# Moving the third group's logs forward and interleaving the first group's second layer in a gated-attention and feed-forward kernel

## Chip, cores and metric

One Trainium2 chip, one core. The metric is the device time of one execution in microseconds (us). The kernel before was run three times without a profile; one more execution was profiled, and all lines of the trace come from that one. Engines: PE (TensorE, matmul; PEld is its weight load), ACT (ScalarE), DVE (VectorE), POOL (GpSimd), SP (SyncE, which issues most DMAs).

## The reference

Two blocks. The first is a recurrence over 768 time steps for 4 batches and 8 heads of dimension 48, with a complex decay per step and channel; the second takes the first's output as 3072 rows of 384 and runs a two-layer network with the activation h cos(h).

```python
mag = np.sqrt(a_re * a_re + a_im * a_im)
scale = np.minimum(mag, 0.999) / (mag + 1e-06)
a_re_n, a_im_n = (a_re * scale, a_im * scale)
for t in range(S):
    new_re = ar * S_re - ai * S_im
    new_im = ar * S_im + ai * S_re
    kv = np.einsum('bhd,bhe->bhde', k[:, :, t], v[:, :, t])
    S_re, S_im = (new_re + kv, new_im)
    y[:, :, t] = np.einsum('bhd,bhde->bhe', q[:, :, t], S_re)
...
h = x @ w_in          # 384 -> 2048
g = h * np.cos(h)
return (g @ w_out)    # 2048 -> 384
```

The inputs q, k, v, a_re, a_im are float32; the two weight matrices arrive as 64-bit floats.

## The kernel before

**Tiling.** The time axis is cut into chunks of 128 steps: 6 per batch, 24 in all (n = 0 to 23). Two chunks make a group (g = 0 to 11). Everything of a group is worked on together: its tiles are 128 steps by 768 values. Within a chunk the recurrence is replaced by attention: with P the running product of the decay's magnitudes and its phase the running sum of its angles, the keys are divided and the queries multiplied by P times cosine and sine, and scores under a causal mask do the rest; a state of 96 x 48 per head passes from chunk to chunk.

**The steps of a group**, by their names in the code:

- `log_steps` (called by `logs`): squares of a_re and a_im on ACT, their sum on DVE, then logarithms and exponentials on ACT with DVE steps between: eight DVE steps in all for groups from 2 on. They end with the tile `tan` (tangent of the half angle) and with the log of the magnitude, which groups from 2 on split into an upper and a lower part (`hi`, `lo`). The last reader of a_re is a check on ACT; after it the a_re and a_im loads of the group after may land, as there is one buffer for each. `logs` yields the logs and then these loads.
- `p_powers`: a running sum over the 128 steps by a matmul with a triangle of ones (PE, `lgs`), one per chunk, then Exp on ACT to P and 1/P (`Q`). In groups from 2 on it takes two records of PE per chunk, for `hi` and `lo`.
- `g_angle`: arctan on ACT, which needs another table of ACT than Ln and Exp.
- `prods`: `g_carry` (adds the last phase of the group before, and splits the angle into `hi` and `lo`), then `p_even` and `p_apply` (DVE: five products; SP: the row DMA of P's last step, and two loads of it).
- `g_phase`: the running sum of angles (PE, `phs`), one per chunk. In groups 0 and 1 the second matmul of a chunk takes the finished phase of the chunk before. ACT casts the sum to a whole number of turns, and DVE subtracts it.
- `keys`: `g_trig` (sine and cosine on ACT; the sine goes where P was, so it waits for the row DMA), `g_stack` (four DVE products to `ks` and `qs`), and then, from group 2 on, `f_transpose` for kT and qT: a DVE transpose of 32 x 32 blocks, then DMAs through DRAM. In group 1 `turned` does it with PE.
- `chunks`: per chunk the scores (`f_scores`, two halves with a DVE mask behind each), the state (`f_state`) and the outputs (`f_out`); at the end `f_xt`, DMAs that bring the group's result into the shape of the network's input `xT`, and the loads of k, q and v for the group after the next.
- `first`: the first layer, `mm1` for jp = 0 to 7. Each unit is six matmuls of 128 x 256 (12 records of PE) into one of three PSUM buffers, then `mm1_gate`: sine and square on ACT, product on DVE. The buffer comes free with the product.
- `second`: the second layer of groups 0 and 1, `mm2(g, i, j0, 4)`: four quarters for each of the two chunks, each quarter four of the 16 blocks of w_out (8 records of PE). Groups from 2 on use another form, with seven products instead (`products`).

**Weights.** w_in and w_out are each fetched in eight raw pieces by POOL's queue into four buffers and converted by `as_floats`: three DVE steps and one of ACT per piece. `convert` makes the steps of this; a piece of w_out (`back`) holds two of the 16 blocks, so a quarter needs two pieces. The raw buffer of a piece comes free when the piece four before it is converted.

**What sets the order.** `weave` takes lists of steps, each with a stretch lo to hi; step i of m gets the place lo + (hi - lo)(i + 0.5)/m, and the steps are emitted in order of place. PE's instructions are chained in the order in which they are emitted (`matmul` and `chain`), and so are ACT's special functions, table loads and squares. The other instructions of ACT and DVE, and the DMAs, are put in order by the scheduler, which works from the order of emission and from when it expects their inputs. On the chip each queue then runs in its compiled order. The change is in the lines from 1284 to 1303, in the function `fast_path`.

Of the kernel before, what the change touches and what calls it, by code (L numbers as in the profile page):

```python
# [487 lines left out]
def fast_path(ctx, tc, q, k, v, a_re, a_im, moe_w_in, moe_w_out, out, least, odd, wide):  # L488
# [11 lines left out]
    G = 2  # L500
# [217 lines left out]
    def cut(t, i, n):  # L718
        return (flat(t) if len(t.shape) == 4 else t)[:, ds(i * DM, n * DM)]
# [116 lines left out]
    def g_angle(g, i, n):  # L836

        at = cut(X[g]["tan"], i, n)
        special(out=at, in_=at, func=AF.Arctan)
# [303 lines left out]
    def products(g, lo, hi):  # L1143
        if g < PLAIN:
            return []
        return [lambda p=p, part=part: seventh(g, p, part)
                for p in range(lo, hi) for part in range(2)]
# [4 lines left out]
    def weave(*parts):  # L1152

        items = []
        for p, (part, lo, hi) in enumerate(parts):
            part = list(part)
            items += [(lo + (hi - lo) * (i + 0.5) / len(part), p, t)
                      for i, t in enumerate(part)]
        for _, _, t in sorted(items, key=lambda x: x[:2]):
            t()  # L1160
# [4 lines left out]
    def keys(g):  # L1165

        if not 0 <= g < NG:
            return
        for i, n in spans(g):
            yield lambda i=i, n=n: g_trig(g, i, n)  # L1170
            yield lambda i=i, n=n: (g_stack(g, i, n), p_end(g, i, n))
            for name in "kT", "qT":
                if g >= PEG:
                    yield lambda i=i, n=n, name=name: f_transpose(g, i, n, name)
# [4 lines left out]
    def powers(g):  # L1179
        return [lambda i=i: p_powers(g, i) for i in range(G)]  # L1180

    def prods(g):
        if not 0 <= g < NG:
            return
        if g not in (1, 2):
            yield from powers(g)
            yield lambda: g_angle(g, 0, G)
        yield lambda: g_carry(g)
        yield lambda: (p_even(g, 0, G), p_apply(g, 0, G))

    def logs(g):
        yield from each(g_log, g)
        if 0 <= g and g + 1 < NG:
            yield lambda: load(g + 1, ("re", "im"))

    def phases(g):
        return [lambda i=i: g_phase(g, i) for i in range(G)] if 0 <= g < NG else []

    def chunks(g):
        for n in range(g * G, g * G + G):  # L1200
            for hh in range(2):
                yield lambda n=n, hh=hh: f_scores(n, hh)
            yield lambda n=n: f_state(n)
            yield lambda n=n: f_out(n)
        yield lambda: f_xt(g)
        if g + 2 < NG:
            yield lambda: load(g + 2, ("k", "q", "v"))

    def first(g):
        order = range(NJ // 2) if g < PLAIN else (0, 4, 1, 5, 2, 6, 3, 7)  # L1210
        return [lambda jp=jp: mm1(g, jp) for jp in order]

    def second(g, i):
        return [lambda j0=j0: mm2(g, i, j0, 4) for j0 in range(0, NJ, 4)] if g < PLAIN else []

    def convert(parts):
        return [lambda dst=dst, src=src: weight(dst, src)() for dst, src in parts]
# [12 lines left out]
    into, back = weight_parts()  # L1230
# [47 lines left out]
    def sums(g, lo, hi):  # L1278
        return [lambda jp=jp: mm1_sums(g, jp) for jp in range(lo, hi)]

    def gates(g, lo, hi):
        return [lambda jp=jp: mm1_gate(g, jp) for jp in range(lo, hi)]

    later = convert(into[RAW:])
    for t in (sums(0, 0, 2) + [lambda: g_angle(1, 0, G)] + later[:1] + gates(0, 0, 1)
              + sums(0, 2, 3) + gates(0, 1, 2) + phases(1) + later[1:2] + gates(0, 2, 3)):
        t()
    weave((first(0)[3:], 0.0, 1.0), (later[2:], 0.0, 0.5), (prods(1), 0.1, 0.12),
          ([lambda: load(2, ("k", "q"))], 0.13, 0.14),
          (keys(1), 0.3, 0.8), (convert(back[:1]), 0.9, 1.0))  # L1290
    over = [t for i in range(G) for name in ("kT", "qT") for t in turned(1, i, name)]
    weave((over, 0.0, 0.2), (chunks(1), 0.2, 1.0), (convert(back[1:4]), 0.1, 1.0))
    weave((second(0, 0), 0.0, 0.25), (convert(back[4:]), 0.0, 0.2), (logs(2), 0.2, 0.21),
          (second(0, 1), 0.25, 0.5), (powers(2), 0.33, 0.36),
          ([lambda: g_angle(2, 0, G)], 0.37, 0.38), (prods(2), 0.38, 0.4),
          (phases(2), 0.44, 0.5), (keys(2), 0.5, 0.65), (first(1), 0.5, 1.0))
    room.close()
    stage.update(pool=ctx.enter_context(tc.tile_pool(name="late", bufs=1)), bufs=1)
    for n in range(2, NG):
        weave((mixes(n - 1, 2, 4), 0.0, 0.12), (logs(n + 1), 0.0, 0.02), (chunks(n), 0.0, 0.36),  # L1300
              (second(n - 1, 0), 0.0, 0.38), (products(n - 1, 0, 3), 0.0, 0.36),
              (prods(n + 1), 0.25, 0.27), (second(n - 1, 1), 0.4, 0.56),
              (products(n - 1, 3, 7), 0.4, 0.56), (phases(n + 1), 0.44, 0.54),
              (keys(n + 1), 0.53, 0.66), (quarters() if n == PLAIN else [], 0.4, 0.9),
              (last_quarter() if n == PLAIN else [], 0.9, 1.0), (first(n), 0.56, 1.0),
              (mixes(n, 0, 2), 0.9, 1.0), (guarded(n - 1, per) if n > 3 else [], 0.1, 0.9))
# [77 lines left out]
```

## Time and profile before

| | us |
|---|---|
| median of 3 runs | 688.53 |
| lowest and highest | 687.56, 688.77 |
| the profiled execution | 685.76 |
| span of its instructions | 684.0 |
| PE busy | 652.7 (95% of the span) |
| DVE busy | 491.0 (72%) |
| ACT busy | 394.0 (58%) |
| POOL busy | 28.9 (4%) |

The granted clock of PE over the whole span is 0.986 of full speed. In a line of a timeline the columns are the start in us from the first instruction, the length in us, the engine, the line of the code (often that of a helper, as L686 for every matmul), the operation, the tile written, the tiles read, their shape and the count of instructions put together; in brackets is how long the engine was idle ahead of it, and what ended that. SPq means SP's own queue of DMA issues. A float32 matmul shows as two records of PE.

The places of the work in the trace: the first layer of group 0 runs from 45 to 72 us, chunks 2 and 3 (group 1) from 72 to 86, the second layer of group 0 with the logs, powers and phases of group 2 from 86 to 122, the first layer of group 1 from 122 to 144, and from there the loop over groups 2 to 11 begins, some 54 us for each.

### The profile page before, as it was taken

The page shows a single profiled execution, that of the slowest core. Times are in us where ns is not written, and L with a number is a line of the kernel's source. Part 1 is how long each engine was busy: PE and PEld are TensorE (multiplying, and loading weights), DVE is VectorE, ACT ScalarE, POOL GpSimd, SP SyncE. Part 2 cuts the span into 40 slices and gives each one's busy share as a digit, 9 for nine tenths or more (in the row PEclk, how much of TensorE's full clock was granted, in tenths as well). Part 3 has the DMA queues.
Part 4 walks back from the last instruction along what each step waited for, and adds up shares of the span by engine and source line. Part 5 has one row for each costly group of instructions (what it writes and reads, how often), then busy time and mean ns, then how long its engine had stood idle before and what let it go on. Part 6 is the DMA issues. An engine that isn't in the chain of part 4 may idle for free.

```text
span 684.0 us, 10721 instructions
## 1 busy us (share of the span) xinstructions
PE 652.7 (95%) x4053; PEld 577.9 (84%) x4053; DVE 491.0 (72%) x793; ACT 394.0 (58%) x728; POOL 28.9 (4%) x47
## 2 busy tenths in 40 slices
PE   7898987979999999999999999999999999999996
PEld 5686944757789989989889989999999999999896
DVE  4999975738768768878768868868768868762241
ACT  6885935474359358459359359359369368342230
POOL 2011100000000001001001000000000000000000
PEclk9999988999999999999999999999999999999999
DMA  9978552453572765675675765665765763363100
GB/s 246 198 195 197 183 161 58 117 126 69 117 184 48 155 170 138 141 185 138 151 174 140 157 168 139 158 168 139 184 140 141 185 149 106 94 145 117 40 6 24
DMA packets 232810, 94.90 MB, mean 139 GB/s; under 512 B 208798, under 2 KB 221217, under 8 KB 232748
## 3 DMA queue, kind: packets, MB, share of 16 engines
q1 hardware_dynamic: 226252, 68.62, 44.5%
q0 software_dynamic: 5632, 25.17, 11.2%
q8 instruction: 34, 0.56, 0.3%
q10 hardware_dynamic: 864, 0.33, 0.2%
q14 instruction: 28, 0.23, 0.1%
HBM read 69.28 MB, written 24.81 MB: 138 GB/s over the span
## 4 chain that ended last, share of the span: by engine, by line
PE 80%; DMA 6%; ACT 6%; DVE 6%; issue 2%; SPq 0%; ACTq 0%; DVEq 0%
PE hp L686 31%; PE op L686 16%; PE sum L686 14%; PE sc L686 6%; PE yp L686 5%; PE sp L686 4%; DMA raw<-in_moe_w_out_dram 3%; PE phs L686 2%; PE lgs L686 1%; DVE mag L675 1%; ACT tan L706 1%; DMA qT<-moved 1%; PE yr L686 1%; DVE w_out L675 1%; ACT rs L706 1%
## 5 line engine op out<-in xcount | busy, mean ns | idle before, releaser
L686 PE MATMUL hp<-xT,w_in 128*128 128x256 f32 x1152 | 251.5, 379 | 1.2 <-DVE gate L675 0.7
L686 PEld LDWEIGHTS hp<-xT,w_in 128*128 128x128 f32 x1152 | 218.3, 190 | 32.2 <-DVE gate L675 1.3
L706 ACT ACTIVATE gate<-hp,half_pi_b 128x512 f32<-128x512 f32 x96 | 65.9, 686 | 125.2 <-PE hp L686 125.2
L686 PE MATMUL op<-w_out,gate 128*128 128x192 f32 (+1 forms) x448 | 109.0, 391 | 3.3 <-DVE w_out L675 3.3
L675 DVE TENSOR_TENSOR gate<-hp,gate 128x512 f32<-128x512 f32 x96 | 65.5, 683 | 55.0 <-ACT junk L675 55.0
L686 PEld LDWEIGHTS op<-w_out,gate 128*128 128x128 f32 x448 | 78.4, 196 | 23.8 <-issue 7.0
L675 ACT ACTIVATE junk<-hp 128x512 bf16<-128x512 f32 x96 | 56.6, 590 | 0.0
L686 PE MATMUL sum<-t_s,s 128*128 128x192 f32 x320 | 55.4, 326 | 0.0
L686 PE MATMUL sc<-qT,kT 96*128 96x128 f32 x384 | 49.4, 276 | 5.5 <-issue 3.9
L686 PEld LDWEIGHTS sc<-qT,kT 96*128 96x128 f32 x384 | 47.5, 192 | 7.8 <-issue 4.5
L686 PEld LDWEIGHTS sum<-t_s,s 128*128 128x128 f32 x320 | 52.5, 190 | 0.3 <-DVE ot L675 0.3
L675 DVE TENSOR_TENSOR atm<-sc,causal 128x512 f32<-128x512 f32 x48 | 33.0, 687 | 23.0 <-PE sc L686 22.9
L675 ACT ACTIVATE ot<-sum 128x192 f32<-128x192 f32 x30 | 9.5, 320 | 49.6 <-PE sum L686 49.6
L686 PE MATMUL yp<-atm,v 128*48 128x128 f32 x352 | 33.6, 277 | 0.7 <-DVE atm L675 0.7
L675 DVE SCALAR_TENSOR_TENSOR ot<-op,ot 128x192 f32<-128x192 f32 x31 | 10.9, 353 | 32.3 <-ACT ot L675 23.7
L702 ACT ACT_TABLE_LOAD x24 | 30.8, 1283 | 4.0 <-DMA ident<-ident_const 3.6
L675 ACT CAST tan<-phs 128x384 int32<-128x384 f32 x24 | 11.5, 478 | 32.1 <-PE phs L686 32.1
L686 PEld LDWEIGHTS sp<-v,ks 128*96 128x96 f32 x320 | 29.7, 165 | 0.0
L686 PE MATMUL sp<-v,ks 128*96 128x48 f32 x320 | 29.6, 245 | 0.0
L686 PE MATMUL yp<-qT,state 96*48 96x128 f32 x304 | 29.6, 272 | 0.0
L686 PE MATMUL sum<-w_out,gate 128*128 128x192 f32 x160 | 29.6, 329 | 0.0
L686 PE MATMUL op<-t_a,gate 128*128 128x192 f32 x160 | 29.0, 332 | 0.0
(138 smaller groups left out, 992.2 us busy)
## 6 DMA issues: line engine op xcount, KB each, us to landing
moved<-tr SPq DMA_DIRECT2D x20, 768.0 KB
raw<-in_moe_w_in_dram POOLq DMA_DIRECT2D x16, 768.0 KB, 5.4
raw<-in_moe_w_out_dram POOLq DMA_DIRECT2D x16, 768.0 KB, 4.9
kT<-moved SPq DMA_DIRECT2D x40, 192.0 KB
qT<-moved SPq DMA_DIRECT2D x10, 768.0 KB
k<-in_k_dram SPq DMA_DIRECT2D x24, 192.0 KB
q<-in_q_dram SPq DMA_DIRECT2D x24, 192.0 KB
v<-in_v_dram SPq DMA_DIRECT2D x24, 192.0 KB
```

Source lines behind the costliest of these rows:

```text
L675: ins = getattr(self.engine, op)(**kw)
L686: chain(nc.tensor.matmul(out, **kw), "tensor")
L702: chain(nc.scalar.preload_act_table_set(table))
L706: chain(nc.scalar.activation(func=func, **kw))
```

## The change

Four things, all in the order of emission; no instruction is added or left out.

1. Opening: the phase sum of group 1's first chunk (`phases(1)[:1]`) is emitted ahead of the first gate and of the third unit's sums, instead of behind the second gate; that of the second chunk stays behind the second gate.
2. `logs(2)` (with the loads of group 3's a_re and a_im behind it) goes from the second layer of group 0, at 0.2, into the weave of group 1's chunks, at 0.7: behind the scores of chunk 3 and ahead of its state.
3. The two chunks of group 0's second layer are interleaved in quarters (`both`): first quarter of chunk 0, first quarter of chunk 1, second quarter of chunk 0, and so on. The last four conversions of w_out, group 2's powers, arctan, products, phases and keys get new places. On PE the order becomes: five quarters, power sums, three quarters, phase sums, first unit of group 1's first layer. Before it was: five quarters (four of chunk 0, one of chunk 1), a power sum, a quarter, a power sum, a quarter, a phase sum, a quarter, a phase sum. Both transposes of `keys(2)` are now emitted ahead of the second unit of the first layer; before, the second transpose came behind it, and the sine and cosine came ahead of the first unit's gate.
4. In the loop the second layer of a group's first chunk goes from 0 to 0.38 to -0.08 to 0.28. This concerns group 1 alone, as later groups have no such steps: its first quarter now comes ahead of group 2's first scores, and the others come earlier as well.

```diff
-    for t in (sums(0, 0, 2) + [lambda: g_angle(1, 0, G)] + later[:1] + gates(0, 0, 1)
-              + sums(0, 2, 3) + gates(0, 1, 2) + phases(1) + later[1:2] + gates(0, 2, 3)):
+    for t in (sums(0, 0, 2) + [lambda: g_angle(1, 0, G)] + later[:1] + phases(1)[:1]
+              + gates(0, 0, 1) + sums(0, 2, 3) + gates(0, 1, 2) + phases(1)[1:] + later[1:2]
+              + gates(0, 2, 3)):
         t()
...
-    weave((over, 0.0, 0.2), (chunks(1), 0.2, 1.0), (convert(back[1:4]), 0.1, 1.0))
-    weave((second(0, 0), 0.0, 0.25), (convert(back[4:]), 0.0, 0.2), (logs(2), 0.2, 0.21),
-          (second(0, 1), 0.25, 0.5), (powers(2), 0.33, 0.36),
-          ([lambda: g_angle(2, 0, G)], 0.37, 0.38), (prods(2), 0.38, 0.4),
-          (phases(2), 0.44, 0.5), (keys(2), 0.5, 0.65), (first(1), 0.5, 1.0))
+    weave((over, 0.0, 0.2), (chunks(1), 0.2, 1.0), (convert(back[1:4]), 0.1, 1.0),
+          (logs(2), 0.7, 0.71))
+    both = [t for pair in zip(second(0, 0), second(0, 1)) for t in pair]
+    weave((both, 0.0, 0.5), (convert(back[4:]), 0.0, 0.3), (powers(2), 0.3, 0.34),
+          ([lambda: g_angle(2, 0, G)], 0.35, 0.36), (prods(2), 0.36, 0.4),
+          (phases(2), 0.47, 0.53), (keys(2), 0.53, 0.6), (first(1), 0.5, 1.0))
...
-              (second(n - 1, 0), 0.0, 0.38), (products(n - 1, 0, 3), 0.0, 0.36),
+              (second(n - 1, 0), -0.08, 0.28), (products(n - 1, 0, 3), 0.0, 0.36),
```

## The prediction

> **What bounds the kernel now.** I count groups and chunks from zero: the second group is group 1, and it has chunks 2 and 3. The profiled execution took 685.76 us: a span of 684.0 and 1.76 around it. It lies 2.77 below the median of the runs, 688.53, so I make the sum against 685.76 and add 2.77 at the end. I read the busy time by stretch first.
>
> ```profile
> 86.00:122.20 36.20, 28.89 (x78) 15.68 (x75) 23.81 (x30) 15.73 (x23) 1.19 (x1) 0.86 0.39 107
> 122.20:148.00 25.80, 21.32 (x98) 17.91 (x96) 15.23 (x19) 14.56 (x30) 0.00 (x0) 1.00 0.66 154
> ...
> 182.20:236.00 53.80, 53.80 (x347) 49.98 (x346) 42.27 (x65) 31.11 (x59) 0.00 (x0) 1.00 0.51 117
> ...
> 100.00:105.00 5.00, 5.00 (x9) 2.55 (x8) 2.39 (x3) 3.69 (x6) 0.00 (x0) 0.54 0.11 39
> ```
>
> The columns are the stretch, its length, each engine's busy time, then the granted TensorE clock. From 182.2 on PE is busy all of the 53.80 us of a group, so that part is bound by PE and whatever is won earlier reaches the end. The stretch from 86.0 to 122.2 (the second layer of group 0) holds 28.89 us of PE work in 36.20 us, part of that at a clock of 0.54; from 122.2 to 148.0, 21.32 us in 25.80. The time that can be had lies here. The order of PE's work over time says where:
>
> ```profile
> 57.80 0.91 PE L686 MATMUL phs<-tan,last 128*128 128x384 f32 x2 [2.88 <-DVE tan L675]
> 58.55 13.28 PE L686 MATMUL hp<-xT,w_in 128*128 128x256 f32 x60
> ...
> 86.12 8.01 PE L686 MATMUL op<-w_out,gate 128*128 128x384 f32 x24
> 96.88 2.07 PE L686 MATMUL op<-w_out,gate 128*128 128x384 f32 x4 [2.75 <-DVE w_out L675]
> 99.48 6.67 PE L686 MATMUL op<-w_out,gate 128*128 128x384 f32 x12 [0.53 <-DVE w_out L675]
> ...
> 115.98 0.44 PE L686 MATMUL phs<-hi,exact 128*128 128x384 f32 x1 [2.06 <-ACT hi L675]
> ...
> 117.27 4.33 PE L686 MATMUL op<-w_out,gate 128*128 128x384 f32 x8
> ...
> 122.22 10.52 PE L686 MATMUL hp<-xT,w_in 128*128 128x256 f32 x48
> 133.40 10.78 PE L686 MATMUL hp<-xT,w_in 128*128 128x256 f32 x48 [0.65 <-DVE gate L675]
> 148.07 1.21 PE L686 MATMUL sc<-qT,kT 96*128 96x128 f32 x8 [3.90 <-issue]
> 149.08 4.40 PE L686 MATMUL op<-w_out,gate 128*128 128x384 f32 x8
> 153.31 1.06 PE L686 MATMUL sc<-qT,kT 96*128 96x128 f32 x8
> ...
> 157.44 0.43 PE L686 MATMUL yp<-atm,v 128*48 128x128 f32 x4 [0.74 <-DVE atm L675]
> ```
>
> The columns are start, time to the end of the piece, instruction and count; in brackets the idle time ahead. PE waits 2.88 us for a phase at 57.80, 2.75 for converted w_out at 96.88, 2.06 for the upper half of group 2's angle at 115.98, and 3.90 at 148.07 (the profile names no releaser; the scores read keys and queries that come by DMA). The clock adds to that: 24 records of a quarter type take 8.01 us at 86.12, 0.334 each, but 12 take 6.67 at 99.48, 0.556 each. A quarter (four of the sixteen blocks of a chunk) is 8 records, 2.67 us.
>
> Then VectorE, ScalarE and the queues of SyncE and GpSimd, which have to feed these places:
>
> ```profile
> 32.52 0.94 DVE L675 TENSOR_TENSOR lg<-lg,tan 128x768 f32<-128x768 f32 x1
> ...
> 48.29 0.95 DVE L675 SCALAR_TENSOR_TENSOR tan<-tan,im 128x768 f32<-128x768 f32 x1
> ...
> 56.59 0.69 DVE L675 TENSOR_TENSOR gate<-hp,gate 128x512 f32<-128x512 f32 x1 [0.92 <-ACT junk L675]
> 57.20 0.55 DVE L675 TENSOR_TENSOR tan<-phs,tan 128x384 f32<-128x384 f32 x1
> ...
> 65.32 0.95 DVE L675 CUSTOM_DVE_ANT_0 w_in<-raw,w_in 128x1536 uint16<-128x1536 uint16 x1
> ...
> 95.40 0.56 DVE L675 TENSOR_SCALAR w_out<-raw 128x768 uint32<-128x768 uint32 x1 [2.05 <-DMA raw<-in_moe_w_out_dram]
> ...
> 97.61 0.95 DVE L675 TENSOR_TENSOR lg<-lg,tan 128x768 f32<-128x768 f32 x1
> 98.48 0.95 DVE L675 CUSTOM_DVE_ANT_0 w_out<-raw,w_out 128x1536 uint16<-128x1536 uint16 x1
> ...
> 106.96 0.95 DVE L675 SCALAR_TENSOR_TENSOR lo<-lg,hi 128x768 fp32r<-128x768 f32 x1
> ...
> 108.81 0.96 DVE L675 SCALAR_TENSOR_TENSOR tan<-tan,im 128x768 f32<-128x768 f32 x1
> ...
> 126.29 0.96 DVE L675 TENSOR_TENSOR ks<-Q,lg 128x768 f32<-128x768 f32 x1 [2.13 <-ACT lg L706]
> ...
> 130.45 2.24 DVE L675 STREAM_TRANSPOSE tr<-ks 128x1536 f32<-128x1536 f32 x1
> ...
> 133.27 2.24 DVE L675 STREAM_TRANSPOSE tr<-qs 128x1536 f32<-128x1536 f32 x1
> ```
>
> ```profile
> 79.09 0.89 ACT L743 ACTIVATE tan<-im 128x768 f32<-128x768 f32 x1
> ...
> 111.38 0.49 ACT L706 ACTIVATE lg<-lgs 128x384 f32<-128x384 f32 x1 [2.06 <-PE lgs L686]
> ...
> 125.41 0.84 ACT L706 ACTIVATE lg<-tan 128x768 f32<-128x768 f32 x1 [2.51 <-DMA row<-lg]
> ```
>
> ```profile
> 86.84 1.19 SPq L1007 DMA_DIRECT2D x<-yT  x2
> ...
> 91.06 0.38 SPq L1011 DMA_DIRECT2D xT<-x  x1
> ...
> 106.05 2.04 SPq L567 DMA_DIRECT2D re<-in_a_re_dram  x4
> ...
> 122.80 0.55 SPq L818 DMA_DIRECT2D row<-lg  x1
> ...
> 140.76 1.30 SPq L911 DMA_DIRECT2D qT<-moved  x1
> ```
>
> ```profile
> 88.37 1.19 POOL L616 DMA_DIRECT2D raw<-in_moe_w_out_dram  x1 [3.33 <-DVE w_out L675]
> ```
>
> Group 2's squares are done on ScalarE at 79.98, but VectorE adds them only at 97.61, after nearly all of the weight conversion: 17.6 us in which the logs could have run. Their eight VectorE steps then last until 109.77, and powers, arctan, phases and first layer all stand behind that. The last raw piece of w_out is asked for at 88.37, lands at 95.40, and is converted at 99.43.
>
> **The change, part by part.**
>
> *Opening.* The first chunk's phase sum goes ahead of the third unit of the first layer (a unit is 12 records, 10.52 / 4 = 2.63 us). While PE does that unit, ScalarE's cast and VectorE's subtraction are made, so the wait of 2.88 at 57.80 goes. What is late next is VectorE: the 60 records from 58.55 are five units, the fourth of which starts at 58.55 + 3 x 2.63 = 66.4, and the conversion of its weights ends at 66.27. That unit had 0.1 us to spare, so PE cannot move up by 2.9 unless VectorE does. VectorE gets back its idle 0.92 at 56.59 (the gate there stands behind less), and the 0.55 of the subtraction at 57.20 moves to an earlier place: I take 1.5, between 0 (the idle time only moves) and 2.9. Everything to 86.12 comes 1.5 earlier: the second layer starts at 84.6.
>
> *Logs.* Nothing is added; eight VectorE steps (seven of 0.95, one of 0.55, 7.2 us by duration, about 0.08 less each back to back) and ScalarE's special functions move from 97.6 onwards to 78.5 onwards, among the masks and conversions. The nearest row for a log stage beside conversions is group 1's own: first addition at 32.52, last step ending at 49.24, 16.7 us. By that group 2's logs end at 78.5 + 16.7 = 95.2; by group 2's own 12.2 us (97.61 to 109.77) at 90.7. They are not wanted before the power sums, at 99.0 by the next part, so both ends cost nothing directly. What they cost is VectorE time: conversions behind them come up to 6.6 us later, less the wait of 2.05 ahead of 95.40, which they fill: 99.43 - 1.5 + 6.6 - 0.9 (the addition stood ahead already) - 2.05 = 101.6 for the last piece.
>
> The loads of the next group's a_re and a_im are moved with the logs. They wait on SyncE's in-order queue for the last reader of a_re. Behind that queue stand the two writes of x and the read of xT (91.06). If the ten issues (about 0.5 each, by the four at 106.05) got ahead of x, x would leave near 100 and xT, 4.2 behind it (86.84, 91.06), near 104; the first layer wants it at 110.3, and the nearest transfer bound, queries asked for at 140.76 and used at 148.07, is 7.3 us. That could cost 1; I expect x to be placed first, because its data are ready when the chunk ends, at about 85, ten us ahead of the logs' end, and cost it at nothing.
>
> *Second layer interleaved.* Same 64 records; 10 records of power and phase sums stand among them, of the same 128x384 shape. At 0.334 that is 24.7 us instead of the 36.10 from 86.12 to 122.22. A quarter of w_out is now used twice before the next is needed, so the needs are spread: order of PE is five quarters, power sums, three quarters, phase sums. Start 84.6; five quarters, 98.0; I add 1.0 of waits for a conversion (0 to 5), 99.0; power sums 1.3, 100.3; the seventh quarter needs the seventh piece at 103.0 and the last piece at 104.3, against 101.6 above: 2.7 to spare where PE waited 2.75 before. Three quarters end at 108.3. The powers' Exp began at 111.38 and the angle's sum at 115.98: 4.6. So its operand is there at 104.9, under cover of those quarters by 3.4, and the wait of 2.06 goes. Phase sums 2.0: the first layer of group 1 starts at 110.3 instead of 122.22. Of these 11.9 us, 10.4 are this part's.
>
> *Keys of group 2 and first layer of group 1.* Sin ran at 125.41, 9.4 us after the angle's operand; it waits for the row DMA that stands at 122.80 behind the moved k and q loads on SyncE. That chain is kept: 104.9 + 9.4 = 114.3. Key products 0.9 later, 115.2 (126.29 against 125.41); four products of 0.95, 3.5 us back to back, and then, as the change puts both transposes ahead of the second unit's gate, 2 x 2.2 us (130.45, 133.27): 123.1. The second gate follows, done at 123.8. The fifth unit needs its buffer and would start at 110.3 + 4 x 2.63 = 120.8: a new wait of 3.0, where 133.40 shows 0.65 now. The eight units end at 123.8 + 10.5 = 134.3. A quarter of group 1's second layer now fills the place where PE waited 3.90: 137.0. From the end of the queries' transpose (135.51) to the scores (148.07) it is 12.6 us: 123.1 + 12.6 = 135.7, so the scores no longer wait. They take 1.0: 138.0. Before, scores and that quarter were both done at 153.31. Gain so far 15.3, of which 3.4 are this part's. What the clock does at the new wait is open. After the wait of 2.88 the 60 records ran in 13.28, 0.221 each, full speed; after 2.75 and 0.53 close together, 12 records lost 12 x 0.222 = 2.7. I take 0.5, nearer the single wait.
>
> The Trainium skill, "TensorE: Matmul & The Clock Gate", section "Why this matters for your kernels", says to leave no gap above some 3 us between matmul bursts, since an idle window halves the clock; it speaks against the new wait. The trace agrees in kind: 0.54 behind the waits of 2.75 and 0.53. An estimate from that page's window of 3.4 us, run at half rate, is a price of 1.7; the forecast would then be 1.2 higher.
>
> *Group 1's second layer.* Three quarters come earlier among the scores. The wait of 0.74 for a mask at 157.44 is covered by a quarter that now stands between scores and outputs: 0.6.
>
> Sum: 1.5 + 10.4 + 3.4 - 0.5 + 0.6 = 15.4; 685.76 - 15.4 = 670.4, and with 2.77, **673.1**.
>
> **The rivals.**
>
> *VectorE becomes the bound (0.20).* Its queue is in order: if its log steps stand there waiting for ScalarE, conversions move by the log stage's 12.2, not by 6.6: the last piece at 107.2 where 104.3 is wanted, a wait of 2.9, with 2.7 for the clock. For it: at 95.40 the conversion of one piece waited for the DMA of the next. Against: conversions that are ready can be queued in the gaps. Gain 9.8: 678.7.
>
> *The change does not do what it says (0.08).* The steps were emitted early enough on ScalarE before, and VectorE still took the addition at 97.61. If the compiled order leaves them there, the power sums wait in PE's order for the lower half, ready at 107.91 - 1.5 = 106.4 instead of 99.0: 7.4 and 2.7 of clock. Gain 5.3: 683.2. Against: the logs are now emitted ahead of the last five conversions.
>
> *More than that (0.11).* The opening gives all 2.9, no conversion waits and the second gate gets ahead of a transpose: 15.4 + 1.4 + 1.0 + 1.5 = 19.3: 669.2.
>
> *The clock stays down: slower (0.05).* Place: the interleaved quarters. If short waits for conversions recur, one per quarter, all 74 records run at 0.556 (+16.4) and the first four units at the same ratio (+7.0): 8.0 slower than before, 696.5. It decides from 69 slow records on, which cancel the 15.4. For it: 99.48, 117.27 (8 in 4.33) and 149.08 (8 in 4.40) all ran slow after waits. Against: each lasted 7 us at most.
>
> Other mishaps that cancel the gain within 0.2% (some 1.4 us, about what a measurement of this kernel can tell from no change): 0.03. The forecast keeps 0.53.
>
> **How the numbers follow.** Forecast 673.1, its own range 670 to 676.5 (opening 0 to 2.9, waits 0 to 4). The range to hold 8 in 10 takes in the better case and VectorE's, and leaves out the last three, 0.16: 668.5 to 680.5. Faster takes the first three and the undone one: 0.53 + 0.20 + 0.11 + 0.08 = 0.92; same 0.03; slower 0.05.
>
> **What would show it.** Right: logs' addition on VectorE near 79 to 84; no PE wait above 1 us between 85 and 110; the first layer of group 1 starting near 110; a wait near 3 us ahead of its fifth unit with both transposes ahead of the second gate; the quarter ahead of the first scores of group 2, and these at 136 to 138; the opening's wait gone but only 1 to 2 us won at the end of that first layer (58.55 + 13.28 = 71.8 before). Wrong: w_out or the logs' halves named as releasers of PE waits above 3 us, the clock below 0.8 in two stretches of 5 us in a row, or a start of that first layer after 114.

## The result, and the profile after

The changed kernel takes 670.64 us (median of 4 runs, 669.56 to 672.38) against 688.65 us (median of 4, 687.56 to 689.14): ratio 0.9743, with a 95% interval of 0.9717 to 0.9769. It is 18.0 us faster. The profiled execution of the changed kernel took 672.38 us, its span is 670.6; so the two profiles differ by 13.4, less than the medians. The profiled execution before (685.76) lies 2.9 below its kernel's median, that of after (672.38, the longest of its four) 1.7 above; 13.4 + 2.9 + 1.7 = 18.0. Why they spread is told below.

PE's order over time in the changed kernel, from the opening to the first scores of group 2 (start, length, instruction, count; in brackets the idle time ahead and what ended it):

```profile
56.03 0.91 PE L686 MATMUL phs<-tan,last 128*128 128x384 f32 x2 [0.63 <-DVE tan L675]
56.77 7.93 PE L686 MATMUL hp<-xT,w_in 128*128 128x256 f32 x36
65.09 2.83 PE L686 MATMUL hp<-xT,w_in 128*128 128x256 f32 x12 [0.38 <-DVE w_in L675]
69.23 2.83 PE L686 MATMUL hp<-xT,w_in 128*128 128x256 f32 x12 [1.31 <-DVE w_in L675]
71.89 1.04 PE L921 MATMUL tp<-ident,ks 128*96 128x128 f32 x8
...
85.93 10.59 PE L686 MATMUL op<-w_out,gate 128*128 128x384 f32 x32
96.82 1.56 PE L686 MATMUL op<-w_out,gate 128*128 128x384 f32 x4 [0.30 <-DVE w_out L675]
99.89 1.56 PE L686 MATMUL op<-w_out,gate 128*128 128x384 f32 x4 [1.52 <-DVE w_out L675]
...
110.76 10.52 PE L686 MATMUL hp<-xT,w_in 128*128 128x256 f32 x48
124.18 12.31 PE L686 MATMUL hp<-xT,w_in 128*128 128x256 f32 x48 [2.89 <-DVE gate L675]
...
138.91 1.95 PE L686 MATMUL sc<-qT,kT 96*128 96x128 f32 x16
```

Four things are to be seen. The opening's wait of 2.88 is down to 0.63, but two units now wait 0.38 and 1.31 for converted w_in, and the first transposes start at 71.89 (71.66 before). The second layer of group 0 runs from 85.93 with waits of 0.30 and 1.52 and never at a low clock (32 records in 10.59 us, 0.331 each). The first layer of group 1 starts at 110.76 where it started at 122.22. And the new wait of 2.89 ahead of its fifth unit is there, with 48 records in 12.31 us behind it where the first 48 took 10.52. The clock over that place (stretch, length, the engines' busy time, then the granted clock):

```profile
120.00:125.00 5.00, 2.11 (x10) 1.53 (x10) 5.00 (x6) 1.26 (x3) 0.00 (x0) 1.00 0.52 214
125.00:130.00 5.00, 5.00 (x17) 4.11 (x16) 0.52 (x2) 1.26 (x3) 0.00 (x0) 0.66 1.11 228
```

VectorE shows, in the opening, group 1's last key product (71.34), then the moved logs (84.00 to 97.62) among the conversions, the last of which ends at 104.0, and then the keys with both transposes ahead of the second gate (123.48, the first of three gates shown in one line):

```profile
71.34 0.95 DVE L675 TENSOR_TENSOR qs<-mag,lg 128x768 f32<-128x768 f32 x1
...
84.00 0.95 DVE L675 TENSOR_TENSOR lg<-lg,tan 128x768 f32<-128x768 f32 x1
...
96.68 0.94 DVE L675 SCALAR_TENSOR_TENSOR tan<-tan,im 128x768 f32<-128x768 f32 x1
...
103.05 0.96 DVE L675 CUSTOM_DVE_ANT_0 w_out<-raw,w_out 128x1536 uint16<-128x1536 uint16 x1
...
119.14 2.23 DVE L675 STREAM_TRANSPOSE tr<-ks 128x1536 f32<-128x1536 f32 x1
...
121.36 2.19 DVE L675 STREAM_TRANSPOSE tr<-qs 128x1536 f32<-128x1536 f32 x1
123.48 1.83 DVE L675 TENSOR_TENSOR gate<-hp,gate 128x512 f32<-128x512 f32 x3
```

In the kernel before, the last key product of group 1 stood at nearly the same time:

```profile
71.33 0.94 DVE L675 TENSOR_TENSOR qs<-mag,rs 128x768 f32<-128x768 f32 x1
```

SyncE's queue shows what the moved loads did:

```profile
87.27 2.58 SPq L1007 DMA_DIRECT2D x<-yT  x2
91.87 0.65 SPq L564 DMA_DIRECT2D re<-in_a_re_dram  x1
...
100.62 0.40 SPq L1011 DMA_DIRECT2D xT<-x  x1
...
109.04 0.25 SPq L818 DMA_DIRECT2D row<-lg  x1
...
110.90 1.11 SPq L567 DMA_DIRECT2D k<-in_k_dram  x2
```

The writes of x left first, at 87.27, but the loads of a_re and a_im then stood ahead of the read of xT, which was asked for at 100.62 instead of 91.06. The row DMA, on the other hand, stood ahead of the loads of k.

Where the 13.4 us between the profiles came from, by PE's marks:

| stretch | before | after | won | forecast |
|---|---|---|---|---|
| to the start of the second layer | 86.12 | 85.93 | 0.2 | 1.5 |
| to the first layer of group 1 | 36.10 | 24.83 | 11.3 | 10.4 |
| to the first half of group 2's first scores and a quarter, both done | 31.09 | 29.0 | 2.1 | 2.9 |
| to the first layer of group 2 | 28.94 | 28.0 | 0.9 | 0.6 |
| the rest of the span | 501.75 | 502.8 | -1.0 | 0 |

The scores of a chunk are sixteen records; before the change the second eight stood behind the quarter, so the forecast and the third row count the first eight alone: the row's end is 153.31 before and 138.91 + 0.89 (half of the time to the next work at 140.69) = 139.8 after. The last row's -1.0 is no effect of the change that can be told from noise: in two profiles of one and the same kernel below (the loop's edit undone), the rest of the span is 500.8 and 503.3. The last two rows rest on the start of group 2's first layer, in the kernel before and in the changed one:

```profile
182.25 20.88 PE L686 MATMUL hp<-xT,w_in 128*128 128x256 f32 x96
```

```profile
167.80 20.94 PE L686 MATMUL hp<-xT,w_in 128*128 128x256 f32 x96
```

### The profile page after: what moved, and what is told of

Read it like the earlier page. It is cut to its first block, busy times and chain, and to the rows that moved or that the text cites. A ratio compares the mean times of both kernels' runs of the same rounds, so it can differ in the third digit from the quotient of the medians.

```text
span 670.6 us, 10717 instructions
## 1 busy us (share of the span) xinstructions
PE 646.9 (96%) x4053; PEld 576.6 (86%) x4053; DVE 490.2 (73%) x793; ACT 392.9 (59%) x728; POOL 28.6 (4%) x47
## 4 chain that ended last, share of the span: by engine, by line
PE 78%; DMA 8%; DVE 7%; ACT 4%; issue 1%; SPq 0%; ACTq 0%; DVEq 0%
PE hp L686 33%; PE op L686 15%; PE sum L686 13%; PE sc L686 5%; PE yp L686 5%; PE sp L686 3%; DMA qT<-moved 2%; DMA raw<-in_moe_w_out_dram 2%; PE phs L686 2%; DMA re<-in_a_re_dram 1%; DVE mag L675 1%; DVE tan L675 1%; PE lgs L686 1%; DMA im<-in_a_im_dram 1%; DMA raw<-in_moe_w_in_dram 1%
## 5 line engine op out<-in xcount | busy, mean ns | idle before, releaser
L686 PE MATMUL op<-w_out,gate 128*128 128x192 f32 (+1 forms) x448 | 102.6, 375 | 1.8 <-DVE w_out L675 1.8
L686 PEld LDWEIGHTS op<-w_out,gate 128*128 128x128 f32 x448 | 75.8, 190 | 19.4 <-DVE w_out L675 3.0
```

Of the source, the lines that this page charges most:

```text
L686: chain(nc.tensor.matmul(out, **kw), "tensor")
```

## The experiments

Four kernels undo one part each. They ran on one chip, where the kernel before took 688.99 (median of 11). Intervals are those of the ratio to the kernel before on the same chip.

**The opening undone.**

```diff
-    for t in (sums(0, 0, 2) + [lambda: g_angle(1, 0, G)] + later[:1] + phases(1)[:1]
-              + gates(0, 0, 1) + sums(0, 2, 3) + gates(0, 1, 2) + phases(1)[1:] + later[1:2]
-              + gates(0, 2, 3)):
+    for t in (sums(0, 0, 2) + [lambda: g_angle(1, 0, G)] + later[:1] + gates(0, 0, 1)
+              + sums(0, 2, 3) + gates(0, 1, 2) + phases(1) + later[1:2] + gates(0, 2, 3)):
```

> The changed kernel with the opening alone put back (both phase sums of group 1 behind the second gate). Theory of the forecast: the opening is worth 1.5 us, so 672.1 against 670.6. Rival, from the trace of the changed kernel: PE reaches the first transposes at 71.89 there and 71.66 before, since the last two units of the first layer wait 0.38 and 1.31 us for converted w_in; VectorE sets this stretch, the opening is worth 0 (within 0.5), so 670.6, and the idle of 2.9 comes back at the phase sum while the waits for w_in go.

Measured: 671.23 us, ratio 0.9744 (0.9714 to 0.9773), against 0.9743 for the changed kernel. The times cannot tell 0 from 1.5, as each ratio is known to 0.003, some 2 us. The profile says what the opening does not win and what it guards against:

```profile
58.64 0.91 PE L686 MATMUL phs<-tan,last 128*128 128x384 f32 x2 [3.06 <-DVE tan L675]
59.39 14.80 PE L686 MATMUL hp<-xT,w_in 128*128 128x256 f32 x60
```

The idle time is back at the phase sum (3.06), and the waits for w_in are gone, as the rival has it. But in this execution the clock fell behind the wait: the 60 records took 14.80 us, where the kernel before needed 13.28 behind its 2.88. So behind this wait one profiled execution lost 1.5 us more, and the other nothing.

**The logs put back.**

```diff
-    weave((over, 0.0, 0.2), (chunks(1), 0.2, 1.0), (convert(back[1:4]), 0.1, 1.0),
-          (logs(2), 0.7, 0.71))
+    weave((over, 0.0, 0.2), (chunks(1), 0.2, 1.0), (convert(back[1:4]), 0.1, 1.0))
...
-    weave((both, 0.0, 0.5), (convert(back[4:]), 0.0, 0.3), (powers(2), 0.3, 0.34),
+    weave((both, 0.0, 0.5), (convert(back[4:]), 0.0, 0.3), (logs(2), 0.2, 0.21), (powers(2), 0.3, 0.34),
```

> The changed kernel with group 2's logs and the loads behind them put back into the weave of group 0's second layer at 0.2; the interleaved quarters stay. Theory: the early logs and the interleaving are needed together; VectorE takes the logs' addition near 95, the lower half is ready near 105, and the power sums, which stand behind five quarters on PE (98.6), wait some 6 us, with 2.7 us for the clock: 9 us slower than the changed kernel, near 680. Rival: the interleaving alone carries the gain by hiding the conversions, and the logs are worth 2 us or less: 673 or below.

Measured: 676.71 us, ratio 0.9839 (0.9808 to 0.9870): 6 to 7 us of the 18 are lost, and the rest stays.

```profile
85.74 13.17 PE L686 MATMUL op<-w_out,gate 128*128 128x384 f32 x40
102.58 0.66 PE L686 MATMUL lgs<-hi,exact 128*128 128x384 f32 x1 [3.68 <-issue]
...
104.79 9.83 PE L686 MATMUL op<-w_out,gate 128*128 128x384 f32 x24
```

The quarters no longer wait for w_out at all (40 records in 13.17 us). The wait is at the power sums, 3.68 and 0.42, and the 24 records behind them take 9.83 us instead of 7.90. Where theory put 6 us of wait and 2.7 of clock, it was 4.1 and 1.9; the rival's 2 us or less is out.

**The quarters in sequence.**

```diff
-    both = [t for pair in zip(second(0, 0), second(0, 1)) for t in pair]
-    weave((both, 0.0, 0.5), (convert(back[4:]), 0.0, 0.3), (powers(2), 0.3, 0.34),
+    both = second(0, 0) + second(0, 1)
+    weave((both, 0.0, 0.5), (convert(back[4:]), 0.0, 0.2), (powers(2), 0.3, 0.34),
```

> The changed kernel with the quarters of group 0's second layer in sequence (four of chunk 0, then four of chunk 1) and the last four conversions of w_out at 0 to 0.2 as before; the early logs stay. Theory: VectorE has logs and conversions to do by the fourth quarter, which PE reaches at 94; the last pieces are converted near 103 to 105, so PE waits some 8 us for w_out, partly at a low clock: 8 to 11 us slower than the changed kernel, near 680. Rival: the early logs alone carry the gain, and sequence costs 2 us or less: 673 or below.

Measured: 678.37 us, ratio 0.9849 (0.9817 to 0.9881): some 7 to 8 us of the gain are lost.

```profile
92.58 1.56 PE L686 MATMUL op<-w_out,gate 128*128 128x384 f32 x4 [1.08 <-DVE w_out L675]
99.02 11.38 PE L686 MATMUL op<-w_out,gate 128*128 128x384 f32 x24 [4.88 <-DVE w_out L675]
```

PE waits 1.08 and 4.88 for w_out, 6.0 where theory put some 8, and 24 records then take 11.38 instead of 7.90, 3.5 for the clock; the rival's 2 us or less is out. So early logs without interleaving press the conversions, and interleaving without early logs leaves the power sums waiting: each part lifts the wait that the other would leave.

**The loop's edit undone.**

```diff
-              (second(n - 1, 0), -0.08, 0.28), (products(n - 1, 0, 3), 0.0, 0.36),
+              (second(n - 1, 0), 0.0, 0.38), (products(n - 1, 0, 3), 0.0, 0.36),
```

> The changed kernel with the first chunk of group 1's second layer back at 0 to 0.38 in the loop, so that no quarter stands ahead of group 2's first scores. Theory, from the trace of the changed kernel: the wait of 2.89 for the second gate holds PE until 136.3, when queries are about ready (transposed at 123.55, and 12.6 us later is 136.2), so the scores wait 0 to 0.5, and a mask wait of 0.7 comes back: 671 to 672. Rival, the forecast's wording that the quarter fills the place of the wait: 2.7 us slower, 673.3.

Measured: 677.03 us, ratio 0.9835 (0.9806 to 0.9864): 6 us slower, more than either view had. But its profiled run was one of 671.29, at a mean clock of 0.994, while the six others took 676.43 to 678.05 at 0.984 to 0.987. The profile of the short run shows 0.93 of wait for the scores and 1.36 for a mask, and no low clock, also not behind the wait of 2.90:

```profile
123.99 10.63 PE L686 MATMUL hp<-xT,w_in 128*128 128x256 f32 x48 [2.90 <-DVE gate L675]
135.55 1.13 PE L686 MATMUL sc<-qT,kT 96*128 96x128 f32 x8 [0.93 <-issue]
...
143.85 0.42 PE L686 MATMUL yp<-atm,v 128*48 128x128 f32 x4 [1.36 <-DVE atm L675]
```

What lies between is taken up below.

The next four kernels ran on a second chip (the kernel before: 686.35, median of 11).

**The loads left behind.**

```diff
-          (logs(2), 0.7, 0.71))
+          (list(logs(2))[:1], 0.7, 0.71))
...
-    weave((both, 0.0, 0.5), (convert(back[4:]), 0.0, 0.3), (powers(2), 0.3, 0.34),
+    weave((both, 0.0, 0.5), (convert(back[4:]), 0.0, 0.3), (list(logs(2))[1:], 0.27, 0.28), (powers(2), 0.3, 0.34),
```

> The changed kernel with the loads of group 3's a_re and a_im back in the second layer's weave; on SyncE's queue the read of xT then stands ahead of all but the first of them. In the changed kernel xT is asked for at 100.62, 9.6 us later than before, behind these loads. Theory: that has cover, as PE wants xT only at 110.76; 670.6, within 0.7. Rival: the loads collide with the last raw pieces of w_out and make the wait of 1.5 ahead of the last conversion: 669 or below.

Measured: 671.17 us, ratio 0.9778 (0.9749 to 0.9807): nothing is won. In its profile xT is asked for at 92.47 (100.62 in the changed kernel), and PE's wait for w_out in the middle of the fifth quarter is 1.52 again, so the loads did not make it. (The expectation calls this the last conversion; two more conversions follow on VectorE.) The 9.6 us by which xT is asked for later had cover.

**The second gate ahead of the transposes** (the first pair of lines), and then **two quarters ahead of the scores** as well (both pairs):

```diff
-          (phases(2), 0.47, 0.53), (keys(2), 0.53, 0.6), (first(1), 0.5, 1.0))
+          (phases(2), 0.47, 0.53), (keys(2), 0.53, 0.65), (first(1), 0.5, 1.0))
...
-              (second(n - 1, 0), -0.08, 0.28), (products(n - 1, 0, 3), 0.0, 0.36),
+              (second(n - 1, 0), -0.2, 0.28), (products(n - 1, 0, 3), 0.0, 0.36),
```

> The changed kernel with the keys of group 2 at 0.53 to 0.65, so that the product of the second gate of group 1's first layer stands on VectorE ahead of both transposes. Theory: the wait of 2.89 ahead of the fifth unit is the price of that order, and the 1.8 us at a low clock behind it come with it; without it the eight units and the quarter end near 134.4 instead of 138.9, the queries come 0.6 later, near 136.8, so a wait of some 2.4 for the scores takes its place: 668.5 (2.1 less). Rival: the transposes bound the stretch anyway, 670.6 or more.

> As gate_first, with the first chunk of group 1's second layer at -0.2 to 0.28, so that two quarters stand ahead of group 2's first scores. Theory: the second quarter fills the wait for the scores that gate_first leaves, and a mask wait of some 0.7 to 1.4 comes where it stood: 667 (1 to 2 below gate_first). Rival: scores are not waited for in gate_first, and this brings nothing or loses the mask wait: 668.5 to 669.5.

Measured: 670.13 us, ratio 0.9757 (0.9733 to 0.9780), and 669.20, ratio 0.9747 (0.9723 to 0.9770). Both ratios lie inside the changed kernel's interval. The profiles say more than the times: with the gate ahead, PE's wait at that place is 0.96 instead of 2.89 and the clock stays at 1.00 from 120 to 140 us, and the scores wait only 0.45 (at 135.71) where theory had 2.4. The measured 670.13 lies between theory's 668.5 and the rival's 670.6. With two quarters, 669.20 is in the range of that run's rival (668.5 to 669.5), not theory's 667. A comparison with the changed kernel in one set of runs follows below.

**The w_in conversions ahead of the products.** The second of these kernels with:

```diff
-    weave((first(0)[3:], 0.0, 1.0), (later[2:], 0.0, 0.5), (prods(1), 0.1, 0.12),
+    weave((first(0)[3:], 0.0, 1.0), (later[2:], 0.0, 0.12), (prods(1), 0.1, 0.12),
```

> As gate_first_two_quarters, with the last two conversions of w_in emitted at 0 to 0.12 in the opening's weave, ahead of group 1's products. Theory: the opening is bound by VectorE's total, not by which of its steps comes first; the waits of 0.38 and 1.31 for w_in go, but the first transposes wait for the keys instead: no change against gate_first_two_quarters within 0.7. Rival: the conversions alone are in the way, and 1.7 is won.

Measured: 669.41 us, ratio 0.9752 (0.9729 to 0.9775), against 669.20 without it in the same set of runs: no difference, as theory had it.

```profile
56.46 13.11 PE L686 MATMUL hp<-xT,w_in 128*128 128x256 f32 x60
71.21 1.08 PE L921 MATMUL tp<-ident,ks 128*96 128x128 f32 x8 [1.64 <-DVE ks L675]
```

The five units run through without a wait (60 records in 13.11), and the transposes wait 1.64 and 1.26 for the keys instead. So PE's wait goes to whatever of VectorE's work comes last, as it would if VectorE's total binds the opening. (VectorE's last key product ends later here, at 73.49 against 72.29 in the changed kernel: it idles 0.74 for ScalarE, and two steps for w_out, 1.02, have come ahead of it.)

**The last four, on the second chip again, as a later set of runs** (the kernel before: 687.07, median of 10): the changed kernel, the undone loop once more, the same with idle matmuls in two waits, and the kernel with two quarters.

The third has, beside the loop's edit undone:

```diff
-          (phases(2), 0.47, 0.53), (keys(2), 0.53, 0.6), (first(1), 0.5, 1.0))
+          (phases(2), 0.47, 0.53), (keys(2), 0.53, 0.6), (first(1), 0.5, 1.0), ([lambda: busy(10)], 0.75, 0.751))
+    busy(4)
```

> The changed kernel itself, on the chip of the next three, so that these are compared at one place: ratio to the kernel before 0.974, within its interval of 0.972 to 0.977.

> The changed kernel with the loop's edit undone, once more: its profiled run took 671.3 us at a clock of 0.994, its six others 676.4 to 678.1 at 0.984 to 0.987. Theory (clock): what this edit removes is mainly time at a low granted clock, as waits of 2.9, 0.9 and 1.4 us follow each other within 25 us; the time is again some 6 us above the changed kernel on the same chip, with a clock lower by near 0.009, and a profile of such a run shows stretches of 0.5 to 0.8 between 120 and 150 us. Rival (waits alone): the waits add 1 to 2 us, and the rest was that chip: 1 to 2 us above.

> The same kernel with idle matmuls in two of the waits: ten of 128x512 (0.25 us each by the profile of the kernel before, 2.5 together) between the fourth and the fifth unit of group 1's first layer, and four behind its eighth. They compute nothing that is used. Theory (clock): the clock stays up, and the time falls to within 1.5 us of the changed kernel, 4 to 6 below the kernel without the filling. Rival (waits alone): waits and end stay as they are, no change, or 0 to 1 us slower for the matmuls themselves.

> The kernel with the second gate ahead of the transposes and two quarters ahead of the scores, against the changed kernel on one chip. Theory: its trace reaches the same work some 2 to 3 us earlier (the wait of 2.9 is 1.0, without the low clock behind it), so 1.5 to 3 us below the changed kernel. Rival: its ratio to the kernel before, 0.9747, equals that of the changed kernel, 0.9743, so nothing is gained, within 0.7.

| kernel | median us | runs | ratio (95%) | mean clock of its runs |
|---|---|---|---|---|
| changed kernel | 671.49 | 671.10 to 673.46 | 0.9774 (0.9742 to 0.9807) | 0.990 to 0.994 |
| loop undone | 676.97 | 675.18 to 678.47 | 0.9844 (0.9811 to 0.9877) | 0.985 to 0.991 |
| loop undone, waits filled | 673.58 | 672.34 to 674.99 | 0.9802 (0.9769 to 0.9834) | 0.991 to 0.995 |
| two quarters | 668.48 | 667.27 to 670.92 | 0.9730 (0.9695 to 0.9764) | 0.992 to 0.995 |

The changed kernel's 0.9774 is at the upper edge of what was expected. The loop's edit is worth 5.5 us here. This time the profile is of a run that has the loss:

```profile
123.94 12.31 PE L686 MATMUL hp<-xT,w_in 128*128 128x256 f32 x48 [2.90 <-DVE gate L675]
...
145.50 0.67 PE L686 MATMUL yp<-atm,v 128*48 128x128 f32 x4 [2.53 <-DVE atm L675]
...
147.37 5.04 PE L686 MATMUL op<-w_out,gate 128*128 128x384 f32 x8
...
145.00:150.00 5.00, 4.50 (x20) 3.01 (x21) 5.00 (x8) 3.04 (x6) 0.00 (x0) 0.50 0.43 82
```

The four units behind the 2.90 run slow (12.31), then PE waits 2.53 for a mask, and behind that the clock is 0.50: a quarter takes 5.04 us instead of 2.75. Why the mask is late stands on VectorE:

```profile
142.18 0.96 DVE L675 SCALAR_TENSOR_TENSOR mag<-re,mag 128x768 f32<-128x768 f32 x1 [1.56 <-ACT mag L706]
...
143.88 0.96 DVE L675 TENSOR_TENSOR lg<-lg,rs 128x768 f32<-128x768 f32 x1 [0.27 <-ACT rs L706]
144.76 0.68 DVE L675 TENSOR_TENSOR atm<-sc,causal 128x512 f32<-128x512 f32 x1
```

The second mask (144.76) stands in the queue behind log steps of group 3 that wait 1.56 and 0.27 for ScalarE, although its scores were done by 140.6. With the changed order both scores run together, and the masks come ahead of those steps (140.16 to 141.58 in the changed kernel, the first of those steps at 142.41).

The two profiles of this one kernel, 671.29 and 678.47 us, are the cleanest comparison of the clock here, as the order is the same in both. The first layer of group 1 starts at 110.57 and 110.53, the first layer of group 2 at 168.66 and 173.36. Of the 4.7 us between them, 1.65 are there when the outputs behind the second mask begin (143.85 and 145.50): the units are 1.7 slower, which takes up the wait of 0.93 for the scores but pushes VectorE's gates and log steps back, so that the mask's wait is 1.2 longer. The other 3.05 come behind the mask, in the rest of the outputs and the quarter, at the clock of 0.50.

What the loop's edit is worth has to be read behind the eight units, as the changed kernel's own units also run slow behind its 2.89 (12.31). From the end of the units to the first layer of group 2 the changed kernel takes 31.5 us (136.33 to 167.80), the undone loop 34.0 at full clock (134.62 to 168.66) and 37.3 in the slower execution (136.10 to 173.36). The 2.6 at full clock are mainly the waits of 0.93 and 1.36. The 5.8 are the mask's wait of 2.53 and the 3.05 of clock behind it: about half each. So theory is right that the loss comes back with low clock between 120 and 150 us (the rival's 1 to 2 us is out), but the time at a low clock is about half of what the edit removes, not the main part.

With idle matmuls in the waits, the profile shows 0.64 where it was 2.90 and a clock of 1.00 from 110 us on:

```profile
120.71 2.64 PE L686 MATMUL busy<-idle 128*128 128x512 f32 x10
123.99 10.63 PE L686 MATMUL hp<-xT,w_in 128*128 128x256 f32 x48 [0.64 <-DVE gate L675]
...
142.62 0.43 PE L686 MATMUL yp<-atm,v 128*48 128x128 f32 x4 [0.37 <-DVE atm L675]
```

```profile
141.89 0.68 DVE L675 TENSOR_TENSOR atm<-sc,causal 128x512 f32<-128x512 f32 x1
142.49 0.95 DVE L675 TENSOR_TENSOR lg<-lg,rs 128x768 f32<-128x768 f32 x1
```

The time falls by 3.4 of the 5.5 us, and the fifth unit begins no earlier (123.99 against 123.94). But this is no measure of the clock's share in what the loop's edit wins, for two reasons. The ten matmuls stand at the wait ahead of the fifth unit, and the units behind it, now at 10.63, ran slow in the changed kernel too: that 1.5 to 1.7 us is not the loop's. And in the compiled order of VectorE the second mask came one log step earlier (141.89, ahead of the step at 142.49): PE waits 0.37 for it where the unfilled kernel waited 1.36 at full clock, so up to 1.0 can be that order, and more if the shorter wait alone would have kept the clock up behind it, which was not tested. Theory had 4 to 6 and a time within 1.5 of the changed kernel; it came to within 2.1. What these 2.1 are is not settled: in the profiles of these last runs it starts group 2's first layer at 167.85, and the changed kernel at 167.98.

The kernel with two quarters is 3.0 us below the changed one, with no run of either inside the range of the other, as theory had it (1.5 to 3); the rival, no gain, is out.

```profile
110.88 13.11 PE L686 MATMUL hp<-xT,w_in 128*128 128x256 f32 x60
124.95 8.04 PE L686 MATMUL hp<-xT,w_in 128*128 128x256 f32 x36 [0.96 <-DVE gate L675]
132.82 5.32 PE L686 MATMUL op<-w_out,gate 128*128 128x384 f32 x16
137.98 1.95 PE L686 MATMUL sc<-qT,kT 96*128 96x128 f32 x16
```

The wait of 2.89 is now 0.96 (ahead of the sixth unit, for the third gate), nothing behind it is slow, and the scores need no wait at 137.98, with one quarter more already done.

## Why the prediction was right, point by point

The forecast was 673.1 (668.5 to 680.5); 670.64 lies inside, and faster was the likeliest case. How near the number came is in part luck. The sum was 15.4 us; between the profiles 13.4 were won, with terms off both ways (0.9 and 0.3 more than forecast, 1.3, 0.8 and 1.0 less), and between the medians 18.0, as the two profiled executions lay on opposite sides of their medians.

Of the signs that were named, these came: the logs' addition at 84.00, the first layer of group 1 at 110.76, the wait of 2.89 ahead of its fifth unit with both transposes ahead of the second gate, the quarter ahead of the scores. These did not: PE waited 1.52 at 99.89, where no wait above 1 was to come; the scores started at 138.91, not at 136 to 138; and nothing was won by the end of the opening, where 1 to 2 us were to be. No sign of being wrong came: no such wait above 3 us, and the clock below 0.8 in one stretch of 5 us alone (0.66).

*Opening: mis-sized.* "I take 1.5, between 0 and 2.9." It was the lower end: 0.2 in the profiles. The step that failed is that VectorE "gets back its idle 0.92": the idle time only moved (0.66 and 0.68 at the two phase subtractions), and VectorE ended group 1's last key product at 72.29 (71.34 + 0.95), to 0.02 us as before (71.33 + 0.94). PE's five units gained 1.8 at their start and gave it back waiting for w_in. With the conversions ahead of the products PE's wait only moved to the keys, so another order of VectorE's steps did not help. What the forecast left out is the other worth of the edit: without it a wait of about 3 us stands there, behind which the clock fell in one profile of two.

*Logs and interleaving: right in kind.* The logs ran from 84.00 to 97.62 (90.7 to 95.2 was the bound, from a start at 78.5; the addition came later, at 84.00, as from 78.5 on VectorE took three masks, a state and conversions first). The last piece was converted at 104.0, where 101.6 was worked out, and PE waited 1.8 where 1.0 was taken. Still this part won 11.3, not 10.4, since 0.334 per record was too high for the ten power and phase sums (2.3 us instead of 3.3) and a little high for the quarters (20.7 instead of 21.4). Both single undoings show that neither edit carries the 11.3 alone; the forecast summed them as one part and had not priced them singly.

*SyncE's queue: another order, same price.* The forecast had x first and took the cost as nothing. The writes of x were first, but xT itself stood behind the loads and was asked for 9.6 us later; PE wanted it 10.1 us after that. The run with the loads left behind shows the same time.

*Keys: the time right, a reason wrong.* Sine was worked out for 114.3 and ran at 114.71, but not because of the row DMA, which now stood ahead of the k loads: issued at 109.04, it would be there near 111.7 by the 2.6 us that lay between issue and sine before (122.80 to 125.41). The rows of ScalarE, in the changed kernel:

```profile
113.55 0.69 ACT L706 ACTIVATE gate<-hp,half_pi_b 128x512 f32<-128x512 f32 x1 [2.11 <-PE hp L686]
...
114.71 0.84 ACT L706 ACTIVATE lg<-tan 128x768 f32<-128x768 f32 x1
```

The first gate's sine (113.55) is chained ahead of it. The new wait came as forecast, 2.89 for 3.0, at 124.18.

*The clock: mis-sized.* 0.5 was taken behind that wait; 48 records lost 1.8. The estimate of 1.7, from the window of 3.4 us that the Trainium skill's page "TensorE: Matmul & The Clock Gate" states (section "Part 1: The HAM clock gate (the "warmup" mystery)"), was the better one for the profiled run. But of the nine such waits of 2.88 to 3.06 in the profiles here the clock fell behind seven (48 records in 12.31 four times, in 12.07 and in 13.63; 60 in 14.80) and not behind two (48 in 10.63 with the loop undone, 60 in 13.28 before). A wait of 3.17 with the logs put back also had 48 records in 12.27 behind it. So the price was mostly 1.5 to 1.8, sometimes nothing, where 0.5 is neither. This fits what the same section of the Trainium skill says, that the window over which the activity is judged runs freely, though no trace here shows that window.

*Group 1's second layer: mis-sized.* I gave the loop's edit 0.6 and the quarter ahead of the scores a share in 3.4. On one chip the loop's edit alone is worth 5.5 us. The forecast took it that without the edit the mask's wait stays 0.74; with the log steps compiled ahead of the mask it was 1.36 in one profile and 2.53 in the other, and behind the 2.53 the clock fell. The step that failed is the mask's wait, taken at 0.74 and with nothing for the clock behind it: it was 2.53, with 3.05 of clock behind it.

*Why the medians differ by more than the profiles.* The kernel before ran at a mean clock of 0.986 in its profile. Its 32 runs in the three sets of experiments have 0.977 to 0.991; with 0.983 or less they mostly took 686 to 690 us, with 0.986 or more mostly 684 to 686. The changed kernel's ten runs have 0.990 to 0.996. It removes most of the waits behind which the clock fell, and it is likely that a sum made against one of the shorter executions misses part of that; this is argued from the spread, not shown. The mean clock of a run is a rough guide at best: one run with the loop undone took 676.32 us at 0.991, and the changed kernel took 671.54 at 0.990. How much of the 18.0 is clock in all was not measured by itself.

Of the rivals, VectorE as the bound was near at the last conversions (1.5 us of wait) and no further; the undone and the slower case did not come. The slower case's mechanism, waits that keep the clock down, is real, and showed with the loop undone, but two waits above 2.5 us cost some 5 us of clock there (1.8 in the units, 3.05 behind the mask), not 23.

## What to carry to other kernels

Where PE waits for two chains at once (here converted weights and logs, both fed by VectorE), price an edit together with the one that frees the other chain: without either of the two, 6 to 8 of the 18 us were lost. Lifting one wait on an engine that is short of time can move it to the next consumer, as in the opening here; look for the engine's last step of the stretch, and if that does not move, nothing is won. And cost a wait of about 3 us on PE as itself plus a chance of low clock behind it: with useful work in its place (the gate ahead of the transposes, two quarters ahead of the scores) the clock stayed at 1.00 here, and with idle matmuls too.

## What the runs showed of the hardware

Waits of PE of 2.88 to 3.06 us were followed by 1.5 to 3.1 us of lost time at a low clock in seven places and by none in two, one and the same kernel (the loop undone) among both. A wait of 2.53 that came some 20 us behind one of 2.90 was followed by a clock of 0.50 over 5 us (a quarter in 5.04 us instead of 2.75). With idle matmuls in two of the waits, 0.26 us each (10 in 2.64), the clock was 1.00 in the profile and the kernel 3.4 us faster, though 1.0 us or more of that can be a mask that came earlier in VectorE's order. Two profiles of one kernel, 671.29 and 678.47 us, differ by 4.7 us between the starts of group 1's and group 2's first layers, in the same order of work, one with the clock at 1.00 throughout and one with stretches of 5 us at 0.71, 0.50 and 0.82.
